# An f32 attention and two feed-forward layers on one core: batches 0 and 1 take the first layer in two rounds of 8 feature tiles, and GpSimd is preferred for the low halves

## The chip, the cores and the metric

The kernel runs on one core of a Trainium2 chip. The metric is the device time of one execution in microseconds (us). A core has five engines that matter here: TensorE (PE, matrix products), VectorE (DVE), ScalarE (ACT), GpSimd (POOL), and SyncE (SP), which here only issues transfers (DMA). Each engine works through its own instructions in the order in which they were written; semaphores hold an instruction back until what it needs is done, and all behind it on that engine wait with it.

## What is computed

For each of 4 batches (8 heads, 576 positions, head dimension 64) a Nystrom attention is formed; its result, 2304 tokens of 512, goes through two feed-forward layers with 2048 hidden features:

```python
A  = sm(q, k_lm);  Bm = sm(q_lm, k_lm);  C = sm(q_lm, k)     # softmax; _lm: means over 18 positions
Z  = Bm.T / (norm1(Bm) * norminf(Bm) + 1e-06)
for _ in range(6):
    Z = 2 * Z - Z @ Bm @ Z
x  = A @ Z @ C @ v                       # to (2304, 512)
h  = x @ w_in;   x = (h * cos(h)) @ w_out                       # first layer
h  = x @ w_in2;  x = (max(h, 0) + alpha * min(h, 0)) @ w_out2   # second layer
```

The weights of both layers are given as 64-bit floats, and the kernel turns them into 32-bit floats itself.

## The kernel before

**Precision.** Most large products are made from values split into a high half (rounded to TensorE's fast 32-bit form by an ACT copy) and a low half (value minus high half). Three products (high-high, high-low, low-high) make one. The subtraction that makes a low half is one two-input instruction on DVE or on POOL: line 323 (`sub`), whichever engine the planner picks.

**Weights.** A conversion (`convert`) takes a 128 x 512 piece. SP loads its raw words (512 KB) into one of three `raw` buffers (L464); DVE joins them by three instructions (L470, L472, L474). A piece of `w_in` then stays in one of eight `wi` buffers and is also written to a DRAM copy `w1d` (L497); a piece of `w_out` is split into halves (ACT L454, low half L323). The first layer needs 16 pieces of each, 32 conversions; 32 more make DRAM copies of the second layer's weights while the first layer runs.

**Attention.** Each batch has two `unit`s (two pairs of heads in each) and one `z_path` (the inverse). A unit of batch 1 to 3 loads k, q and v through the same three `raw` buffers (L551, L567, L568), transposes on PE (L593), takes landmark sums on DVE (L641), makes scores (L658), exponentials (L680), and C v (L703). `z_path` begins with small products (L767), iterates (L839, L852), and ends with L866. Its result goes with converted `w_in` into V' (`vprime`: PE L897, ACT L899, DVE L900), a 512 x 2048 matrix for each batch that stands for Z C v w_in. V' of batch 0 reads the `wi` buffers straight from the conversions; V' of the later batches reloads the pieces from `w1d` (L883).

**First layer.** It runs in 128 ticks (`tick`). A tick is one batch, one half of its positions (`ch`, 288 columns) and one tile of 128 features (`j`): the first product h (L937, six matmuls), ACT and DVE steps for h cos h (L942, L944, L946, L947, L948), its split (ACT L951, L323), and the second product (L964, twelve matmuls), which adds up over a round of feature tiles in four PSUM banks. At the end of a round the sums are written to the DRAM array `y1d` (L991); a second round loads the earlier sums (L977) and adds (L984). In batch 0 a round has 8 tiles, so its order is half 0 tiles 0-7, half 1 tiles 0-7, half 0 tiles 8-15, half 1 tiles 8-15. Batches 1 to 3 take one round of 16 tiles for each half. The table of ticks:

```python
ticks = [(0, ch, j) for jg in range(0, NF, JG) for ch in range(2) for j in range(jg, jg + JG)]
ticks += [(b, ch, j) for b in range(1, NB) for ch in range(2) for j in range(NF)]
```

with `NF` = 16 and `JG` = 8. Ticks 0 to 31 belong to batch 0, 32 to 63 to batch 1, and so on.

**Second layer.** It runs in chunks of 512 tokens with a seven-product scheme (L1208) and the products L1289, and the last chunk of 256 tokens plainly (L1253).

**What sets the order.** No order is written by hand. `Plan.go` goes through all operations with made-up durations (functions `pe`, `act`, `dve`, `pool`), due times (`tick_time`) and buffer slots, and writes each engine's instructions in the order that comes out. Constants stand in the table `KN`. Where an operation may go to DVE or POOL, it goes where the made-up end is earlier, less a bonus for POOL (`PB`). The work of a batch's attention is let in at a tick named in `KN` (`U0`), and the second layer's conversions begin at tick `C2`, one every `CD` ticks. A buffer tag has a fixed number of slots, used in turn, so that the raw piece number n waits until piece n-3 has been read.

Of the kernel before, what the change touches and what calls it, by code (L numbers as in the profile page):

```python
# [18 lines left out]
KN = dict(T0=46, TA=3.4, TBT=3.05, VE=4.0, U0=6, UD=7, UZ=24, C2=36, CD=2.6, LA=4, SW=6.0, BL=0.9, PB=0.2, AB=0.2, LM=126, JG=8, VG=8, AG=8, KA=0.004, KC=25, DRY=0)  # L19
# [239 lines left out]
def kernel(  # L259
# [13 lines left out]
    NB, H, S, D = q.shape  # L273
# [34 lines left out]
    def pool(n):  # L308
        return ("POOL", n / 480.0 + 0.15)
# [82 lines left out]
    g = Plan(place, rounded)  # L392
# [51 lines left out]
    valloc, cvops = [], []  # L444
    T0, TA, TBT = KN["T0"], KN["TA"], KN["TBT"]

    def tick_time(s):
        return T0 + TA * min(s, 2 * NF) + TBT * max(0, s - 2 * NF)
# [30 lines left out]
    gates = {}  # L479
# [436 lines left out]
    h1op = {}  # L916
# [4 lines left out]
    def tick(s):  # L921
        b, ch, j = ticks[s]
        T = tick_time(s)
        fb = j // 4
# [28 lines left out]
        jg = NF if b else JG  # L953
# [41 lines left out]
    LA = KN["LA"]  # L995
# [25 lines left out]
    n2 = 0  # L1021
    for s in range(NTK):
        b = s // (2 * NF)
        if s and s % (2 * NF) == 0:
            for fb in range(NFB):
                for c in range(2):
                    vprime(b, fb, c, tick_time(vfirst[b, fb]) - KN["VE"])
        tick(s)
        if s % (2 * NF) == KN["U0"] and b + 1 < NB:
            gates["ld"] = [h1op[s]]  # L1030
            t = 2 * NF * b
            for c in range(2):
                unit(2 * b + 2 + c, tick_time(s + KN["UD"] * (c + 1)))
            z_path(b + 1, tick_time(t + KN["UZ"]))
            gates["v"] = [g.ops[-1]]
# [6 lines left out]
    for (b, fb), o in vload.items():  # L1042
        o.after.append(h1op[max(0, vlast[b - 1, fb] - KN["VG"])])
# [311 lines left out]
```

## Time and profile before

| | |
|---|---|
| median of 3 runs | 901.36 us (897.68 to 902.41) |
| profiled execution | 894.15 us, span 892.3 us |
| PE busy | 829.2 us (93% of the span) |
| DVE busy | 643.4 us (72%) |
| ACT busy | 488.7 us (55%) |
| POOL busy | 167.9 us (19%) |

The span reaches from the first to the last instruction of the profiled execution; its time is 1.85 us longer. Busy shares are means over stages that are limited by different things, so the stages have to be read one by one: the 45.8 us before the first tick, the 128 ticks (45.8 to 495.5 us), and the second layer (495.5 to 892.3 us). The ticks' times are the starts of the first of their six matmuls on L937: tick 0 at 45.8 us, tick 4 at 58.9, tick 16 at 112.0, tick 24 at 159.0, tick 32 at 187.8, tick 64 at 295.8, tick 96 at 406.6.

### The profile page before, as it was taken

The page shows a single profiled execution, that of the slowest core. Times are in us where ns is not written, and L with a number is a line of the kernel's source. Part 1 is how long each engine was busy: PE and PEld are TensorE (multiplying, and loading weights), DVE is VectorE, ACT ScalarE, POOL GpSimd, SP SyncE. Part 2 cuts the span into 40 slices and gives each one's busy share as a digit, 9 for nine tenths or more (in the row PEclk, how much of TensorE's full clock was granted, in tenths as well). Part 3 has the DMA queues.
Part 4 walks back from the last instruction along what each step waited for, and adds up shares of the span by engine and source line. Part 5 has one row for each costly group of instructions (what it writes and reads, how often), then busy time and mean ns, then how long its engine had stood idle before and what let it go on. Part 6 is the DMA issues. An engine that isn't in the chain of part 4 may idle for free.

```text
span 892.3 us, 15368 instructions
## 1 busy us (share of the span) xinstructions
PE 829.2 (93%) x5681; PEld 728.4 (82%) x5681; DVE 643.4 (72%) x1251; ACT 488.7 (55%) x1132; POOL 167.9 (19%) x176
## 2 busy tenths in 40 slices
PE   6778948899989998999999989999999999999997
PEld 4447726798879887898889978989999998999996
DVE  4989877967798666987888687875565556555562
ACT  4466656667776677767778644443244334333431
POOL 1114211401123111233251122210120012000110
PEclk9899977999999999999999999999999999999999
DMA  8456674636735666558364211131104011310131
GB/s 229 142 189 155 176 235 161 199 100 153 178 121 203 231 131 152 155 195 260 125 203 155 94 47 49 60 104 51 36 32 111 24 36 60 84 36 24 59 119 24
DMA packets 89179, 109.28 MB, mean 122 GB/s; under 512 B 36112, under 2 KB 61200, under 8 KB 89104
## 3 DMA queue, kind: packets, MB, share of 16 engines
q1 hardware_dynamic: 89104, 108.30, 41.0%
q8 instruction: 45, 0.74, 0.3%
q14 instruction: 30, 0.25, 0.1%
HBM read 85.07 MB, written 23.20 MB: 121 GB/s over the span
## 4 chain that ended last, share of the span: by engine, by line
PE 63%; DVE 17%; DMA 9%; ACT 5%; issue 3%; SPq 1%; POOL 1%; DVEq 0%; ACTq 0%; POOLq 0%
PE acc L1289 20%; PE acc L964 12%; PE h L1208 9%; PE x L1208 7%; PE h L937 6%; DMA m<-in_moe_w_in_dram 4%; DMA m<-in_moe_w_out_dram 3%; DVE m L323 2%; DVE m L472 2%; PE x L897 2%; DVE m L474 2%; DVE m L948 2%; DVE m L470 2%; DVE m L944 1%; PE h L1253 1%
## 5 line engine op out<-in xcount | busy, mean ns | idle before, releaser
L964 PE MATMUL acc<-m,m 128*128 128x288 f32 x1536 | 236.5, 301 | 1.4 <-POOL m L323 1.1
L323 POOL TENSOR_TENSOR m<-m,m 128x288 fp32r<-128x288 f32 (+4 forms) x139 | 133.3, 966 | 521.7 <-ACT m L951 259.2
L964 PEld LDWEIGHTS acc<-m,m 128*128 128x128 f32 x1536 | 214.1, 190 | 13.6 <-issue 7.2
L1289 PE MATMUL acc<-m,m 128*128 128x512 f32 x864 | 206.7, 391 | 0.7 <-DVE m L323 0.4
L1289 PEld LDWEIGHTS acc<-m,m 128*128 128x128 f32 x864 | 158.3, 188 | 31.7 <-DVE m L323 0.9
L323 DVE TENSOR_TENSOR m<-m,m 128x512 fp32r<-128x512 f32 (+4 forms) x261 | 159.0, 632 | 32.4 <-ACT m L1157 9.5
L937 PE MATMUL h<-m,m 128*128 128x288 f32 x768 | 131.7, 308 | 15.4 <-DVE m L948 14.3
L937 PEld LDWEIGHTS h<-m,m 128*128 128x128 f32 x768 | 110.9, 193 | 32.4 <-DVE m L948 22.0
L1277 ACT ACTIVATE m<-m 128x512 fp32r<-128x512 f32 (+1 forms) x80 | 46.3, 589 | 111.9 <-DVE m L1275 109.4
L1208 PE MATMUL h<-m,m 128*128 128x256 f32 x768 | 106.5, 281 | 0.8 <-ACT m L318 0.7
L1208 PEld LDWEIGHTS h<-m,m 128*128 128x128 f32 x768 | 99.1, 188 | 3.7 <-ACT m L318 1.4
L1208 PE MATMUL x<-m,m 128*128 128x256 f32 x576 | 80.0, 283 | 1.8 <-ACT m L318 1.8
L1231 DVE TENSOR_TENSOR m<-h,m 128x512 f32<-128x512 f32 x32 | 22.1, 690 | 81.4 <-ACT m L318 78.5
L951 ACT ACTIVATE m<-m 128x288 fp32r<-128x288 f32 x128 | 56.4, 442 | 36.8 <-DVE m L948 34.6
L1208 PEld LDWEIGHTS x<-m,m 128*128 128x128 f32 x576 | 72.9, 188 | 3.5 <-ACT m L318 2.0
L318 ACT ACTIVATE m<-h 128x256 f32<-128x256 f32 (+2 forms) x93 | 36.9, 396 | 69.8 <-PE h L1208 58.3
L948 DVE SCALAR_TENSOR_TENSOR m<-m,h 128x288 f32<-128x288 f32 x128 | 57.1, 447 | 23.0 <-ACT m L947 23.0
L946 ACT ACTIVATE m<-m 128x288 f32<-128x288 f32 x128 | 56.3, 442 | 30.1 <-DVE m L944 29.2
L942 ACT ACTIVATE m<-h 128x288 int32<-128x288 f32 x128 | 51.8, 405 | 25.1 <-PE h L937 24.2
L1068 ACT ACTIVATE m<-m 128x512 fp32r<-128x512 f32 x68 | 41.4, 628 | 43.0 <-PE h L1208 18.7
L944 DVE SCALAR_TENSOR_TENSOR m<-h,m 128x288 f32<-128x288 f32 x128 | 57.4, 450 | 7.6 <-ACT m L942 7.1
L947 ACT ACTIVATE m<-m 128x288 f32<-128x288 f32 x128 | 55.8, 440 | 2.3
(149 smaller groups left out, 874.6 us busy)
## 6 DMA issues: line engine op xcount, KB each, us to landing
m<-in_moe_w_in_dram SPq DMA_DIRECT2D x32, 512.0 KB, 4.9
m<-in_moe_w_out_dram SPq DMA_DIRECT2D x32, 512.0 KB, 4.6
m<-wi2d SPq DMA_DIRECT2D x56, 256.0 KB, 3.3
m<-w1d SPq DMA_DIRECT2D x48, 256.0 KB, 5.0
y1d<-m SPq DMA_DIRECT2D x20, 288.0 KB, 4.2
out_dram<-m SPq DMA_DIRECT2D x36, 128.0 KB, 2.4
w1d<-m SPq DMA_DIRECT2D x16, 256.0 KB, 5.7
wi2d<-m SPq DMA_DIRECT2D x16, 256.0 KB, 2.6
```

What stands on the lines that cost most here:

```text
L323: ENG[e].tensor_tensor(o, a, b, op=ALU.subtract)
L937: nc.tensor.matmul(out=hp.t[:, 0:CW], lhsT=w_[:, js], rhs=x[:, cs], start=(i == 0), stop=(i == 5))
L942: op(act(CW, True), lambda e: nc.scalar.activation(k_.t, hp.t[:, 0:CW], AF.Copy, scale=INV2PI), r=[hp], w=[k_], target=T + 0.8)
L944: op(dve(CW), lambda e: nc.vector.scalar_tensor_tensor(u.t, hp.t[:, 0:CW], INV2PI, k_.t, op0=ALU.mult, op1=ALU.subtract), r=[hp, k_], w=[u])
L946: op(act(CW), lambda e: nc.scalar.activation(u.t, u.t, AF.Sin, scale=math.pi), rw=[u], aset="sin")
L947: op(act(CW), lambda e: nc.scalar.activation(u.t, u.t, AF.Square, scale=math.sqrt(2.0)), rw=[u])
L948: op(dve(CW), lambda e: nc.vector.scalar_tensor_tensor(hc.t, u.t, 1.0, hp.t[:, 0:CW], op0=ALU.subtract, op1=ALU.mult, reverse0=True), r=[h ...
L951: op(act(CW), lambda e: nc.scalar.activation(gh.t, hc.t, AF.Copy), r=[hc], w=[gh, gl])
L964: nc.tensor.matmul(out=yg[o].t[:, 0:CW], lhsT=w_.t[:, sl], rhs=x.t, start=(j == ja and i == 0), stop=(j == jb and i == 2),)
L1208: nc.tensor.matmul(out=rv(k), lhsT=a_.t[:, p, c2, js], rhs=b_.t[:, q_, c2, 0:hw], start=(first and c2 == 0 and i == 0), stop=(c2 == 1 and ...
L1277: op(act(w), lambda e, m_=m_, gh=gh: nc.scalar.activation(gh.t[:, 0:w], m_.t[:, 0:w], AF.Copy), r=[m_], w=[gh, gl])
L1289: nc.tensor.matmul(out=ya[n][t].t, lhsT=gv(x_), rhs=r_.t, start=(st and k == 0), stop=(en and k == 2))
```

## The change

Three things change. Batches 0 and 1 are interleaved in rounds of 8 tiles: tiles 0-7 of batch 0 (ticks 0-15), tiles 0-7 of batch 1 (16-31), tiles 8-15 of batch 0 (32-47), tiles 8-15 of batch 1 (48-63). Attention of batch 1 is let in before tick 0, and V' of both batches is made in two groups that read the conversions' own `wi` buffers, without the reload. The planner's bonus for POOL is 0.8 us instead of 0.2 (with POOL taken to be somewhat slower), and some due ticks are moved.

```diff
-KN = dict(... U0=6, UD=7, UZ=24, C2=36, CD=2.6, ... PB=0.2, ...)
+KN = dict(... U1=-1, U2=36, U3=66, UD=7, UZ=20, C2=48, CD=2.3, ... PB=0.8, ...)
...
     def pool(n):
-        return ("POOL", n / 480.0 + 0.15)
+        return ("POOL", n / 440.0 + 0.3)
...
     def tick_time(s):
-        return T0 + TA * min(s, 2 * NF) + TBT * max(0, s - 2 * NF)
+        return T0 + TA * min(s, 2 * JG) + TBT * max(0, s - 2 * JG)
...
     def vprime(b, fb, c, target):
-        if b:
+        if b > 1:
...
-    ticks = [(0, ch, j) for jg in range(0, NF, JG) for ch in range(2) for j in range(jg, jg + JG)]
-    ticks += [(b, ch, j) for b in range(1, NB) for ch in range(2) for j in range(NF)]
+    ticks = [(b, ch, j) for jg in range(0, NF, JG) for b in range(2) for ch in range(2) for j in range(jg, jg + JG)]
+    ticks += [(b, ch, j) for b in range(2, NB) for ch in range(2) for j in range(NF)]
...
-        jg = NF if b else JG
+        jg = JG if b < 2 else NF
...
+    def attend(b, s):
+        gates["ld"] = [h1op[s]] if s >= 0 else gates["ld"]
+        for c in range(2):
+            unit(2 * b + c, tick_time(s + KN["UD"] * (c + 1)))
+        z_path(b, tick_time(s + KN["UZ"]))
+        gates["v"] = [g.ops[-1]]
+
+    if KN["U1"] < 0:
+        attend(1, -1)
+        vgroup(1, range(FH))
     for s in range(NTK):
-        b = s // (2 * NF)
-        if s and s % (2 * NF) == 0:
-            for fb in range(NFB):
-                for c in range(2):
-                    vprime(b, fb, c, tick_time(vfirst[b, fb]) - KN["VE"])
+        if s == 4 * JG:
+            vgroup(0, range(FH, NFB))
+        if s == 6 * JG:
+            vgroup(1, range(FH, NFB))
+        if s >= 4 * NF and s % (2 * NF) == 0:
+            vgroup(s // (2 * NF), range(NFB))
         tick(s)
```

`vgroup(b, fbs)` calls `vprime` for the named groups of 512 features. The changed file's line numbers are higher by 1 (from L464 on) up to 16 (in the second layer).

How instructions move is seen in three places. The first is SP's list around the last load of the first half of `w_in`, before (m_157 holds the raw buffers, m_419 and m_442 are `wi` buffers):

```order
L464 DMA m_157<-in_moe_w_in_dram 128x1024
L464 DMA m_157<-in_moe_w_out_dram 128x1024 x2
L497 DMA w1d<-m_419 128x512 x2
L497 DMA w1d<-m_442 128x512
L464 DMA m_157<-in_moe_w_out_dram 128x1024
L497 DMA w1d<-m_442 128x512
L464 DMA m_157<-in_moe_w_out_dram 128x1024 x4
L1185 DMA alpha_sb<-in_moe_alpha_dram 128x16x1
L551 DMA m_157<-in_k_dram 64x9x64 x4
```

The same place in the changed kernel (m_408 is a `wi` buffer):

```order
L465 DMA m_157<-in_moe_w_in_dram 128x1024
L552 DMA m_157<-in_k_dram 64x9x64 x4
L465 DMA m_157<-in_moe_w_out_dram 128x1024
L552 DMA m_157<-in_q_dram 64x9x64 x4
L498 DMA w1d<-m_408 128x512
L465 DMA m_157<-in_moe_w_out_dram 128x1024 x2
L568 DMA m_157<-in_v_dram 64x2x320
L569 DMA m_157<-in_v_dram 64x2x256
```

The loads of batch 1's k, q and v have moved ahead of most of the `w_out` pieces: k now stands where the first `w_out` load stood, and seven `w_out` loads came ahead of it before.

The second place is PE's list at the end of batch 1's `z_path`, before (m_207 is a `wi` buffer, m_408 the result of `z_path`, m_415 and m_425 the attention of batch 0):

```order
L852 MATMUL x<-m_69 128x64 x2
L937 MATMUL h<-m_415,m_1011 128x288
...
L866 MATMUL x<-m_69 128x128 x2
L964 MATMUL acc<-m_474,m_1463 128x288 x12
L897 MATMUL x<-m_207,m_408 64x512 x2
L964 MATMUL acc<-m_474,m_1463 128x288 x12
L937 MATMUL h<-m_415,m_1011 128x288
```

and in the changed kernel (m_812 and m_1158 are the attention of batch 1):

```order
L867 MATMUL x<-m_69 128x128 x2
L965 MATMUL acc<-m_485,m_750 128x288 x6
L898 MATMUL x<-m_207,m_410 64x512
L898 MATMUL x<-m_283,m_410 64x512 x2
L898 MATMUL x<-m_207,m_410 64x512
L965 MATMUL acc<-m_485,m_750 128x288 x6
L898 MATMUL x<-m_408,m_410 64x512 x2
L938 MATMUL h<-m_812,m_1240 128x288 x3
L938 MATMUL h<-m_1158,m_1240 128x288 x3
```

Before, the end of `z_path` stands between ticks 25 and 26, and ticks of batch 0 follow it. Now it stands right ahead of tick 16, and no tick of batch 0 is left to run behind it: tick 16 is the first that reads batch 1.

The third place is DVE's list in the changed kernel behind that end (L858 is the last step of the `z_path` on DVE, L901 the low half of V', L471 and L473 the first two steps of a conversion), with what each waits for:

```order
L858 TENSOR_SCALAR m_69<-m_69 128x2x64
L901 TENSOR_TENSOR m_1240<-x,m_1240 128x512 [waits Activation_49]
L471 TENSOR_SCALAR m_207<-m_157 128x512 [waits DMAHW1_49,PE_49]
L901 TENSOR_TENSOR m_1240<-x,m_1240 128x512 [waits Activation_49]
L471 TENSOR_SCALAR m_207<-m_157 128x512 [waits DMAHW2_49]
L471 TENSOR_SCALAR m_283<-m_157 128x512 [waits DMAHW6_49,DMAHW7_49,DMAHW5_49,DMAHW0_49]
L473 SCALAR_TENSOR_TENSOR m_207<-m_157,m_207 128x512 [waits DVE_49]
```

The first conversion of the second half of `w_in` writes the `wi` buffer m_207 and waits for PE, that is for V' of batch 1 to have read it. Before, that buffer was free once V' of batch 0 had read it, near tick 0.

## Rows read from the trace of the kernel before

**Rows 1.** Busy time in stretches: us, PE, PEld, DVE, ACT, POOL, clock, DMA share, GB/s.

```profile
45.80:58.90 13.10, 9.31 (x34) 5.05 (x32) 11.12 (x25) 7.52 (x16) 0.00 (x0) 0.87 0.49 154
58.90:112.00 53.10, 47.52 (x355) 40.65 (x355) 49.30 (x90) 35.95 (x87) 17.86 (x16) 1.00 0.66 181
112.00:159.00 47.00, 29.70 (x208) 21.14 (x206) 37.02 (x81) 29.60 (x65) 8.84 (x9) 0.78 0.61 193
159.00:187.80 28.80, 27.03 (x177) 24.70 (x178) 24.88 (x49) 17.90 (x44) 7.12 (x7) 0.94 0.56 185
187.80:295.80 108.00, 104.02 (x815) 91.64 (x815) 85.46 (x183) 76.43 (x185) 23.52 (x24) 1.00 0.55 157
295.80:406.60 110.80, 105.88 (x817) 93.33 (x816) 84.01 (x181) 80.02 (x194) 23.59 (x25) 0.98 0.61 166
406.60:495.50 88.90, 85.76 (x602) 79.74 (x601) 73.43 (x141) 68.17 (x174) 28.48 (x31) 0.98 0.58 189
495.50:892.30 396.80, 388.46 (x2450) 351.18 (x2448) 245.52 (x420) 153.01 (x330) 52.04 (x51) 1.00 0.19 57
```

**Rows 2.** Waits of PE between 45.8 and 187.8 us: us in total, times, longest.

```profile
PE x L767 <- ACT m L680: 9.0, 1, 9.0
PE h L937 <- DVE m L948: 5.2, 6, 1.3
PE x L688 <- DVE m L900: 3.7, 1, 3.7
```

**Rows 3.** DVE's groups by shape between 45.8 and 187.8 us: count, busy us, mean ns.

```profile
L474 DVE SCALAR_TENSOR_TENSOR m<-m,m 128x512 int32<-128x512 int32 x28 | 22.3, 802 | 0.1
L472 DVE SCALAR_TENSOR_TENSOR m<-m,m 128x512 int32<-128x512 int32 x28 | 20.5, 734 | 0.0
L470 DVE TENSOR_SCALAR m<-m 128x512 int32<-128x512 int32 x27 | 14.0, 523 | 6.3 <-DMA m<-in_moe_w_out_dram 3.9 <-DMA m<-in_moe_w_in_dram 2.4
L948 DVE SCALAR_TENSOR_TENSOR m<-m,h 128x288 f32<-128x288 f32 x31 | 13.7, 446 | 2.5 <-ACT m L947 2.5
L323 DVE TENSOR_TENSOR m<-m,m 128x512 fp32r<-128x512 f32 x12 | 8.2, 685 | 0.6 <-ACT m L454 0.5
L323 DVE TENSOR_TENSOR m<-m,m 128x288 fp32r<-128x288 f32 x8 | 3.5, 453 | 0.6 <-ACT m L951 0.4
```

**Rows 4.** POOL's groups by shape between 45.8 and 187.8 us.

```profile
L323 POOL TENSOR_TENSOR m<-m,m 128x288 fp32r<-128x288 f32 x23 | 23.2, 1012 | 77.6 <-ACT m L951 72.2 <-PE acc L964 2.8 <-issue 2.6
L323 POOL TENSOR_TENSOR m<-m,m 128x512 fp32r<-128x512 f32 x4 | 6.1, 1524 | 11.5 <-DMA w1d<-m 8.7 <-ACT m L454 1.5 <-DMA m<-in_moe_w_out_dram 1.3
```

**Rows 5.** Timelines of DVE, then POOL, 66 to 78 us: start, duration.

```profile
67.44 0.41 DVE L470 TENSOR_SCALAR m<-m 128x512 int32<-128x512 int32 x1
...
68.14 0.68 DVE L472 SCALAR_TENSOR_TENSOR m<-m,m 128x512 int32<-128x512 int32 x1
68.74 1.48 DVE L470 TENSOR_SCALAR m<-m 128x512 int32<-128x512 int32 x1
70.14 1.29 DVE L474 SCALAR_TENSOR_TENSOR m<-m,m 128x512 int32<-128x512 int32 x1
...
68.26 2.63 POOL L323 TENSOR_TENSOR m<-m,m 128x512 fp32r<-128x512 f32 x2 [1.30 <-ACT m L454]
```

**Rows 6.** Timeline of SP: two `w_out` loads, then batch 1's first k load.

```profile
51.65 0.93 SPq L464 DMA_DIRECT2D m<-in_moe_w_out_dram  x2
...
74.25 3.42 SPq L551 DMA_DIRECT2D m<-in_k_dram  x4
```

**Rows 7.** Timeline of PE, 160 to 195 us: end of `z_path`, V', steady ticks.

```profile
166.35 1.06 PE L866 MATMUL x<-m 128*128 128x128 f32 x4
...
169.30 1.27 PE L897 MATMUL x<-m,m 128*64 128x512 f32 x4
...
173.10 1.08 PE L897 MATMUL x<-m,m 128*64 128x512 f32 x4
...
190.13 0.95 PE L937 MATMUL h<-m,m 128*128 128x288 f32 x6
...
192.53 0.95 PE L937 MATMUL h<-m,m 128*128 128x288 f32 x6
```

More of the change, by code (lines that the diff above doesn't have):

```diff
@@ L18 @@
 INV2PI = 1.0 / (2.0 * math.pi)
-KN = dict(T0=46, TA=3.4, TBT=3.05, VE=4.0, U0=6, UD=7, UZ=24, C2=36, CD=2.6, LA=4, SW=6.0, BL=0.9, PB=0.2, AB=0.2, LM=126, JG=8, VG=8, AG=8, KA=0.004, KC=25, DRY=0)
+KN = dict(T0=46, TA=3.4, TBT=3.05, VE=4.0, U1=-1, U2=36, U3=66, UD=7, UZ=20, C2=48, CD=2.3, LA=4, SW=6.0, BL=0.9, PB=0.8, AB=0.2, LM=126, JG=8, VG=8, AG=8, KA=0.004, KC=25, DRY=0)
 ADJ = {}
@@ L444 @@
     valloc, cvops = [], []
+    JG = KN["JG"]
     T0, TA, TBT = KN["T0"], KN["TA"], KN["TBT"]
     def tick_time(s):
-        return T0 + TA * min(s, 2 * NF) + TBT * max(0, s - 2 * NF)
+        return T0 + TA * min(s, 2 * JG) + TBT * max(0, s - 2 * JG)
     def loads(n, fn, dur, r=(), w=(), target=None, after=(), rw=(), hold=()):
@@ L1002, with vgroup @@
     gates["v"] = []
-    for fb in range(NFB):
-        for c in range(2):
-            vprime(0, fb, c, tick_time(vfirst[0, fb]) - KN["VE"])
+    def vgroup(b, fbs):
+        for fb in fbs:
+            for c in range(2):
+                vprime(b, fb, c, tick_time(vfirst[b, fb]) - KN["VE"])
+    FH = JG // 4
+    vgroup(0, range(FH))
     w2c = {}
@@ L1021 @@
     n2 = 0
-    for s in range(NTK):
-        b = s // (2 * NF)
-        if s and s % (2 * NF) == 0:
-            for fb in range(NFB):
-                for c in range(2):
-                    vprime(b, fb, c, tick_time(vfirst[b, fb]) - KN["VE"])
-        tick(s)
[L1029 to L1035, printed above, removed]
+    US = {KN["U1"]: 1, KN["U2"]: 2, KN["U3"]: 3}
+    def attend(b, s):
+        gates["ld"] = [h1op[s]] if s >= 0 else gates["ld"]
+        for c in range(2):
+            unit(2 * b + c, tick_time(s + KN["UD"] * (c + 1)))
[4 more added lines that the diff above has]
+        vgroup(1, range(FH))
+    for s in range(NTK):
+        if s == 4 * JG:
[4 more added lines that the diff above has]
+            vgroup(s // (2 * NF), range(NFB))
+        tick(s)
+        if s in US:
+            attend(US[s], s)
+            if US[s] == 1:
+                vgroup(1, range(FH))
         while n2 < len(w2) and int(KN["C2"] + KN["CD"] * n2) <= s:
@@ L1042 @@
     for (b, fb), o in vload.items():
-        o.after.append(h1op[max(0, vlast[b - 1, fb] - KN["VG"])])
+        o.after.append(h1op[max(0, vlast[b - 1 if b > 2 else 0 if fb < FH else 1, fb % FH + FH if b == 2 else fb] - KN["VG"])])
     HF = DFF // 2
```

## The prediction, made before the changed kernel ran

> **What bounds the kernel now.** I read first the busy times of the stretches between ticks [rows 1]. From tick 32 on PE is what counts: it is busy 104.0 of 108.0 us in ticks 32-63, 191.6 of 199.7 in ticks 64-127, and 388.5 of 396.8 in the second layer. Ticks 0-31 are different. They take 13.1 + 53.1 + 47.0 + 28.8 = 142.0 us, and PE is busy 113.6 of them; ticks 32-63, as many, take 108.0. DVE is busy 11.1 + 49.3 + 37.0 + 24.9 = 122.3 of the 142.0 us, and 49.3 of 53.1 in ticks 4-15, where it is the bound.
>
> Then I read who keeps PE waiting there [rows 2]. The longest wait, 9.0 us, is that of the first product of batch 1's `z_path` for an exponential on ACT; the next single one, 3.7 us, is for a low half of V' on DVE. Both are attention or V' of the next batch standing in PE's list ahead of ticks that could run. The shape groups of DVE [rows 3] say what it works on: 28 conversions in the stretch, at 0.523 + 0.734 + 0.802 = 2.06 us each, are 57 of its 122 us. So in ticks 0-31 the kernel converts the second half of both weights, because tick 16 already needs it, and does the attention of batch 1 beside it.
>
> **What the change takes from DVE in ticks 0-31.** Counted in the order of both kernels, from tick 0's L948 to tick 32's: conversions 25 before, 21 after (the rest follow tick 32); low halves 512 wide on DVE 12 before, 2 after (four more on POOL, six put off with their conversions); low halves 288 wide on DVE 9 before, 11 after. With [rows 3]: -4 x 2.06 - 10 x 0.685 + 2 x 0.453 = -14.2 us.
>
> **What POOL costs in return.** In ticks 0-31 POOL gets four more wide low halves and two fewer narrow ones: 4 x 1.524 - 2 x 1.012 = +4.1 us [rows 4]. This is not free to DVE. L470 takes 0.41 us and L472 0.68 with POOL idle, but L470 takes 1.48 and L474 1.29 while POOL works on two low halves from 68.26 us [rows 5]. Over the stretch the three steps of a conversion are 0.11 + 0.05 + 0.12 = 0.29 us longer than alone (0.41, 0.68, 0.68, L474 taken as L472), 28 times, 8.1 us, for 17.9 + 8.8 + 7.1 = 33.8 us of POOL: 0.24 us of DVE lost for each us of POOL. L948, with an input in PSUM, stays at 0.446 us. So +4.1 us of POOL costs DVE 1.0 us; 4.1 us if all of it blocked, nothing if all fell into DVE's gaps. I take 1.0, the mean of the stretch.
>
> The Trainium skill (SBUF — State Buffer, Who interferes with whom) says that a DVE instruction with two SBUF inputs and a GpSimd one that reads SBUF exclude each other and that the second "fully blocks". The trace agrees where they meet (1.29 against 0.68 us). By it alone, with every moved half blocking, the change would lose most of its gain; that is rival 2.
>
> With DVE's idle time as it is (142.0 - 122.3 = 19.7 us), ticks 0-31 get 14.2 - 1.0 = 13.2 us shorter.
>
> **Which wait is next.** Attention of batch 1 must now end before tick 16, not tick 32, since no tick of batch 0 stands behind it. So I work the stretch out a second way, along that chain. Its first k load now stands where the first `w_out` load stood, issued at 51.65 us; before it was issued at 74.25 [rows 6]. From there to the first V' matmul at 169.30 [rows 7] it took 95 us. Over those 95 us DVE was busy about 0.93 x 37.8 + 37.0 + 0.86 x 10.3 = 81 us [rows 1]. What stands in DVE's list of the changed kernel between the two ends (every instruction at its shape's mean, less 11%, by which neighbours overlapped in those 95 us) comes to about 62 us, 19 less, chiefly because 9 conversions lie there and not 17 (8 x 2.06 = 16.5). If the chain shortens by those 19 us it takes 76, and V' of batch 1 starts at 51.65 + 76 = 128 us. Bounds: 51.65 + 62/0.93 = 118, where DVE's work alone counts, and 51.65 + 95 = 147, where the chain takes as long as now. I take 128, since DVE's queue ended most of the links before. Tick 16 then starts at about 131, behind two V' pairs on PE (1.27 + 1.08 [rows 7]) and a low half on DVE; before it started at 112.0.
>
> Ticks 16-31 then lack nothing but the second half of `w_in`, whose conversion waits for V' of batch 1 to give its buffers back. DVE: 10 conversions (20.6), 16 x 2 steps at 0.446 (14.3), 6 narrow and 3 wide low halves (4.8): 39.7 us, at 0.93 busy 43. PE: 16 x 2.40 (190.13 to 192.53, [rows 7]) + 3 V' pairs at 1.08 = 41.6 us, less some second products that slip behind tick 32. I take 42, so tick 32 starts at 173 and not 187.8: 14.8 us gained. The two ways agree; I take 14.5.
>
> **What is moved later or costs nothing.** Ticks 32-63: 11 conversions lie there before and after, V' and attention of batch 2 too, and PE has the same products to do; it was busy 104.0 of 108.0, so 0, with -4 to +4 as bounds (its idle time gone, or doubled). Batch 1's second round adds 4 loads and 4 stores of `y1d`, and 8 additions on DVE in place of copies (8 x 0.446 = 3.6 us, hidden, since DVE is busy 79% there; without that cover, 3.6). The 16 reloads of `w1d` that go were hidden behind PE. Ticks 64-127: 25 conversions, 21 before (+8.2 us of DVE); 22 more narrow halves on POOL (-10.0 on DVE, +22.3 on POOL, which costs DVE 0.24 x 22.3 = 5.3). DVE gets +3.5 on 157.4 of 199.7 us, with PE idle 8.1: I take +1, bounds -3 and +6. Second layer: two dozen wide halves move to POOL, each 1.524 - 0.685 = 0.84 us later, before products that PE reaches through a queue it is 98% busy with: 0, bounds 0 and +5.
>
> **The sum.** -14.5 + 0 + 1 + 0 = -13.5 us against the profiled execution's 894.15: 880.6. That execution lies 7.2 us below the median of 901.36, so on the scale of the medians: 901.36 - 13.5 = 888.
>
> **Rivals.** *1, larger gain:* DVE packs as well over all of ticks 0-31 as in ticks 4-15 (0.93). 122.3 - 13.2 = 109.1 / 0.93 = 117 us and not 142: -25, so 877. For it: the 13.4 us of the two long waits of PE go if the order is kinder. Against: attention is a serial chain.
>
> *2, no change through POOL:* every moved half blocks DVE for its whole time. Ticks 0-31 then lose 4.1 and not 1.0, and ticks 64-127 22.3 - 10.0 + 8.2 = +20.5 us of DVE, which fills 178 of 199.7 us (89%) and pushes PE by about 8. Sum -11 + 8 = -3, 898. For it the row at 70.14 us; against it the mean of 0.24.
>
> *3, slower:* the chain of batch 1's attention keeps its 95 us. V' starts at 147, tick 16 at 150, tick 32 at 192, 4 us later than now; with +1 behind it, +5, 906. It decides from a V' of about 142 us on. For it: most of its links are waits on other engines, and k, q, v and `w_out` share three raw buffers in turn. Against: DVE has 19 us less ahead of it.
>
> *4:* the gain is there but the moved conversions cost as much in ticks 32-127 (+4 and +6): -14.5 + 10 = -4.5, 897.
>
> **Chances.** Forecast (881 to 894) 0.51; rival 1 (870 to 881) 0.20; rivals 2 and 4 (894 to 900) 0.18; rival 3 0.11. A difference under 0.5% (4.5 us) is about what a measurement of this kernel cannot tell from none. Faster than 896.9: 0.51 + 0.20 + 0.05 of the third case = 0.76; within: 0.13 of it and 0.02 of rival 3 = 0.15; slower 0.09. The range leaves out half of rival 3 and half of rival 1's far end: 874 to 901.
>
> **What would show it.** In the changed profile: tick 16 (the first h that reads batch 1) at 131 us, give or take 8; tick 32 near 173; ticks 16-31 in 40 to 45 us without the clock falling to 0.78; PE's 9.0 us wait on the exponential gone or much shorter; ticks 32-63 in 104 to 112 us; the second layer in 397. POOL's busy time goes up by about 80 us, and L472 and L474 get longer. Wrong would be: a wait of 10 us or more right ahead of V' of batch 1, or ticks 64-127 longer than 204 us.

## The result, and the profile after

Against the kernel before on the same chip the changed kernel took 888.6 us (median of 4, 888.1 to 889.3) where the kernel before took 899.5 (median of 4): a ratio of 0.9896, 95% interval 0.9855 to 0.9936. A second comparison, with more executions (10 of the changed kernel, 33 of the kernel before), gave 891.7 against 898.0, 0.9938 (0.9915 to 0.9962). So the change is faster, by 6 to 11 us (0.6 to 1.0%); 13.5 were predicted.

The first view is that of the busy times between ticks of the changed kernel (888.11 us, span 886.1). Columns as in [rows 1]; the cuts are ticks 0, 4, 16, 32, 64, 96, and the end of the last tick's first steps.

```profile
46.70:58.80 12.10, 8.40 (x36) 4.33 (x35) 10.55 (x21) 7.89 (x18) 0.81 (x1) 1.00 0.55 135
58.80:133.40 74.60, 61.55 (x473) 50.72 (x471) 60.62 (x126) 47.93 (x109) 22.30 (x21) 0.93 0.50 133
133.40:175.70 42.30, 38.45 (x264) 34.17 (x263) 36.47 (x71) 29.17 (x73) 9.91 (x11) 1.00 0.65 203
175.70:285.70 110.00, 105.46 (x817) 91.96 (x816) 92.56 (x191) 84.00 (x199) 33.17 (x34) 1.00 0.53 156
285.70:395.90 110.20, 105.04 (x815) 91.84 (x815) 85.71 (x181) 77.93 (x188) 29.93 (x34) 1.00 0.67 187
395.90:488.10 92.20, 86.81 (x603) 79.91 (x602) 77.26 (x139) 67.97 (x174) 41.26 (x42) 0.98 0.61 200
488.10:886.10 398.00, 389.62 (x2449) 352.66 (x2448) 236.05 (x384) 152.95 (x330) 93.17 (x88) 1.00 0.19 57
```

Read as a balance against [rows 1]: before tick 0 46.7 us against 45.8, +0.9. Ticks 0-31 12.1 + 74.6 + 42.3 = 129.0 against 142.0, -13.0. Ticks 32-63 110.0 against 108.0, +2.0. Ticks 64-95 110.2 against 110.8, -0.6. From tick 96 to the end 92.2 + 398.0 = 490.2 against 88.9 + 396.8 = 485.7, +4.5. The sum is -6.2, the difference of the two spans. Of the 13.0 us that ticks 0-31 gain, 5.9 are spent again behind them.

PE's waits between 46.7 and 175.7 us, to be held against [rows 2]:

```profile
PE h L938 <- DVE m L949: 9.4, 10, 2.2
PE x L594 <- DMA m<-in_q_dram: 3.7, 2, 2.4
PE x L898 <- DVE m L475: 3.0, 2, 1.5
PE x L768 <- DVE m L731: 0.9, 1, 0.9
```

The single wait of 9.0 us ahead of `z_path` is down to 0.9. What has grown are the short waits for the last DVE step of a tick (L949): 9.4 us in ten waits, where [rows 2] has 5.2 in six. Two waits for q of batch 1 make 3.7 us. None is longer than 2.4 us.

DVE's groups by shape in the same stretch, then POOL's, against [rows 3, 4]:

```profile
L473 DVE SCALAR_TENSOR_TENSOR m<-m,m 128x512 int32<-128x512 int32 x23 | 18.2, 800 | 0.1
L475 DVE SCALAR_TENSOR_TENSOR m<-m,m 128x512 int32<-128x512 int32 x22 | 16.8, 776 | 0.0
...
L471 DVE TENSOR_SCALAR m<-m 128x512 int32<-128x512 int32 x21 | 10.4, 500 | 6.6 <-DMA m<-in_moe_w_in_dram 4.2 <-DMA m<-in_moe_w_out_dram 1.2 <-issue 1.1
...
L323 DVE TENSOR_TENSOR m<-m,m 128x288 fp32r<-128x288 f32 x10 | 6.7, 679 | 1.7 <-ACT m L952 1.7
...
L323 POOL TENSOR_TENSOR m<-m,m 128x288 fp32r<-128x288 f32 x21 | 18.6, 891 | 79.3 <-ACT m L952 70.4 <-PE x L689 5.7 <-DMA m<-in_k_dram 2.9
L323 POOL TENSOR_TENSOR m<-m,m 128x512 fp32r<-128x512 f32 x8 | 10.3, 1286 | 15.3 <-ACT m L455 9.8 <-DMA m<-in_q_dram 4.9 <-PE acc L965 0.6
```

Some 22 conversions stand here where 28 stood. A low half of 288 columns takes 0.679 us on DVE on average, but that mean mixes two kinds. The five that POOL's work overlapped for 41 to 76% of their time took 0.53 to 1.32 us; the other five took 0.44 to 0.46, as one does when POOL is idle (0.449, below). Before, none of the eight on DVE met any work of POOL (0.453).

The end of batch 1's chain on PE, against [rows 7]: the first V' product at 129.54 us and tick 16 (L938) at 133.41.

```profile
129.54 1.94 PE L898 MATMUL x<-m,m 128*64 128x512 f32 x8
...
133.41 0.80 PE L938 MATMUL h<-m,m 128*128 128x288 f32 x4
```

### The profile page after: what moved, and what is told of

Same layout as the page of the kernel before. It is cut to its first block, busy times and chain, and to the rows that moved or that the text cites. A ratio compares the mean times of both kernels' runs of the same rounds, so it can differ in the third digit from the quotient of the medians.

```text
span 886.1 us, 15408 instructions
## 1 busy us (share of the span) xinstructions
PE 826.8 (93%) x5681; PEld 726.6 (82%) x5681; DVE 632.6 (71%) x1191; ACT 487.9 (55%) x1132; POOL 239.6 (27%) x246
## 4 chain that ended last, share of the span: by engine, by line
PE 57%; DVE 20%; DMA 10%; ACT 6%; issue 4%; SPq 2%; POOL 1%; DVEq 0%; ACTq 0%
PE acc L1305 21%; PE h L1224 9%; PE acc L965 9%; PE x L1224 7%; PE h L938 4%; DMA m<-in_moe_w_in_dram 4%; DVE m L323 3%; DMA m<-in_moe_w_out_dram 3%; DVE m L473 2%; DVE m L475 2%; DVE m L945 2%; DVE m L949 2%; DVE m L471 2%; PE x L898 1%; ACT m L318 1%
## 5 line engine op out<-in xcount | busy, mean ns | idle before, releaser
L323 POOL TENSOR_TENSOR m<-m,m 128x288 fp32r<-128x288 f32 (+4 forms) x211 | 207.7, 989 | 559.6 <-ACT m L952 240.0
L323 DVE TENSOR_TENSOR m<-m,m 128x512 fp32r<-128x512 f32 (+4 forms) x189 | 138.0, 751 | 26.1 <-ACT m L1173 7.1
L938 PE MATMUL h<-m,m 128*128 128x288 f32 x768 | 129.9, 305 | 21.5 <-DVE m L949 19.3
L938 PEld LDWEIGHTS h<-m,m 128*128 128x128 f32 x768 | 107.7, 188 | 41.0 <-DVE m L949 28.1
L1224 PEld LDWEIGHTS h<-m,m 128*128 128x128 f32 x768 | 100.1, 190 | 6.5 <-ACT m L318 4.1
L949 DVE SCALAR_TENSOR_TENSOR m<-m,h 128x288 f32<-128x288 f32 x128 | 56.8, 446 | 24.6 <-ACT m L948 15.3
```

The lines of the kernel that those rows point to most:

```text
L323: ENG[e].tensor_tensor(o, a, b, op=ALU.subtract)
L938: nc.tensor.matmul(out=hp.t[:, 0:CW], lhsT=w_[:, js], rhs=x[:, cs], start=(i == 0), stop=(i == 5))
L949: op(dve(CW), lambda e: nc.vector.scalar_tensor_tensor(hc.t, u.t, 1.0, hp.t[:, 0:CW], op0=ALU.subtract, op1=ALU.mult, reverse0=True), r=[h ...
L1224: nc.tensor.matmul(out=rv(k), lhsT=a_.t[:, p, c2, js], rhs=b_.t[:, q_, c2, 0:hw], start=(first and c2 == 0 and i == 0), stop=(c2 == 1 and ...
```

## The experiments

Stretches are given as in the balance above: ticks 0-31, 32-63, 64-127 (to the start of tick 127), and from there to the end. For the kernel before they are 141.9, 108.1, 197.3 and 399.2 us. They come from one execution each, the ratios from all; executions of one kernel scatter by some 1%, so a stretch is trusted here where several kernels show the same. Four profiles whose instructions stand in the same order up to tick 32 (the changed kernel twice, and two kernels below that differ from it only later) took 127.3, 129.0, 129.4 and 130.3 us for ticks 0-31. So 3 us in that stretch of a single profile can be scatter.

**The two halves of the change apart.** First the changed kernel once more:

> The changed kernel again, beside the others on one chip. Both theories: 886 to 890 us, 0.985 to 0.993 of the kernel before; its profile with tick 16 at 131 to 136 us and tick 32 at 173 to 178 us.

130.3, 110.1, 202.0 and 399.9 us; 891.7 us, 0.9938. The time, the ratio and tick 32 (178.4 us) each lie just above the range that was expected. Its windows from tick 0 to the end, cut at ticks 16, 32, 64 and 127:

```profile
48.10:135.90 87.80, 72.82 (x508) 57.13 (x506) 70.34 (x146) 55.93 (x126) 23.47 (x22) 0.90 0.50 132
135.90:178.40 42.50, 38.37 (x263) 34.07 (x262) 36.49 (x71) 29.06 (x73) 10.40 (x11) 1.00 0.65 202
178.40:288.50 110.10, 105.59 (x816) 91.94 (x815) 92.31 (x191) 84.05 (x199) 32.99 (x34) 1.00 0.53 156
288.50:490.50 202.00, 188.41 (x1398) 167.90 (x1397) 160.68 (x316) 143.37 (x356) 69.75 (x75) 1.00 0.64 192
490.50:890.40 399.90, 391.00 (x2468) 353.86 (x2466) 236.42 (x387) 155.17 (x335) 94.86 (x90) 1.00 0.20 58
```

Then the rounds with GpSimd's old bonus and price:

```diff
-KN = dict(... PB=0.8, ...)
+KN = dict(... PB=0.2, ...)
-        return ("POOL", n / 440.0 + 0.3)
+        return ("POOL", n / 480.0 + 0.15)
```

> Rounds, early attention and moved conversions as in the changed kernel, but GpSimd's bonus 0.2 us and its made-up cost as before. My theory (the gain is made by the order of ticks 0 to 31, GpSimd moves little): tick 32 within 3 us of the changed kernel's 175.7, time within 4 us of the changed kernel's, so 0.985 to 0.995 of before. Rival (the gain comes from the low halves that DVE no longer makes): tick 32 at 182 or later, time 0.994 to 1.003 of before.

892.6 us, 0.9958 (0.9935 to 0.9982). The windows of this kernel from tick 0 to tick 127:

```profile
44.90:132.80 87.90, 70.90 (x510) 57.37 (x508) 74.23 (x155) 55.77 (x128) 13.75 (x13) 0.92 0.52 132
132.80:178.80 46.00, 40.75 (x260) 36.75 (x259) 39.95 (x80) 30.29 (x74) 9.69 (x9) 0.93 0.63 198
178.80:285.00 106.20, 103.81 (x817) 91.81 (x816) 89.27 (x194) 83.17 (x196) 20.96 (x24) 1.00 0.56 156
285.00:492.50 207.50, 190.05 (x1398) 168.07 (x1397) 169.00 (x340) 147.61 (x360) 53.71 (x57) 1.00 0.63 187
```

The rounds alone shorten ticks 0-31 by 8 us (133.9) and ticks 32-63 by 2, and lengthen ticks 64-127 by 10 (207.5): DVE is busy 169.0 us there, and PE, with the same products as in the other kernels, idles 17. The ratio lies in the rival's range and just outside mine, tick 32 (178.8 us) near mine and far from the rival's. The ratio's interval overlaps that of the changed kernel, so the totals do not show that GpSimd's part adds anything to the rounds.

And GpSimd's part without the rounds (the kernel before, with `PB=0.8` and the new price):

> The kernel before with GpSimd's bonus 0.8 us and its new made-up cost, and no other change. My theory: tick 32 within 4 us of 187.8, time 0.996 to 1.004 of before. Rival (the gain comes from the low halves that DVE no longer makes): tick 32 at 180 or earlier, time 0.993 or less.

900.2 us, 1.0041 (1.0019 to 1.0063): slower, if by little. 139.4, 108.0, 201.7 and 400.2 us: it wins 2.5 us early and loses 4.4 in ticks 64-127. Tick 32 (186.5 us) and the time are where my theory had them. So the gain of the whole change comes from the rounds and what goes with them.

**All low halves on DVE** (`PB=-9.0` in the changed kernel, so that POOL makes only four of them):

> The changed kernel with a malus of 9 us on GpSimd, so that nearly every low half is made on DVE. My theory (a us of GpSimd costs DVE about 0.24 us, so moving a half does pay): the steps of a conversion fall to about 0.41, 0.68 and 0.68 us; DVE gets 7 us more to do in ticks 0 to 31, tick 32 at 179 to 185; ticks 32 to 127 3 to 12 us longer; time 5 to 18 us over the changed kernel's. Rival (a half on GpSimd blocks DVE for its whole time, so moving it gains nothing): tick 32 at 173 to 177, time within 3 us of the changed kernel's.

893.7 us, 0.9955 (0.9933 to 0.9977): 2 us above the changed kernel by the medians, and the intervals overlap. Its windows:

```profile
47.90:135.10 87.20, 73.12 (x515) 58.37 (x515) 74.33 (x164) 54.86 (x133) 1.86 (x2) 0.90 0.54 142
135.10:173.40 38.30, 35.55 (x255) 32.73 (x254) 34.62 (x77) 28.22 (x71) 0.00 (x0) 1.00 0.59 193
173.40:287.50 114.10, 106.65 (x816) 93.78 (x816) 101.09 (x229) 85.83 (x200) 0.00 (x0) 0.97 0.54 158
287.50:496.30 208.80, 190.27 (x1401) 170.57 (x1401) 172.38 (x393) 149.16 (x357) 1.91 (x2) 0.98 0.63 187
496.30:892.40 396.10, 389.43 (x2464) 353.14 (x2463) 251.09 (x472) 155.43 (x337) 0.00 (x0) 1.00 0.20 58
```

I had expected ticks 0-31 to lengthen. They are 5 us shorter than in the changed kernel (125.5 against 130.3, and still 2 us below the shortest of the four above), with DVE busy only 2 us more (108.9 against 106.8). Tick 32, at 173.4, and the total are where the rival had them, not I. But those 5 us are lent: ticks 32-63 take 114.1 us (PE has the same 816 products there, at a granted clock of 0.97 against 1.00), and tick 64 stands 239.6 us behind tick 0, as it does with rounds alone (240.1) and in the changed kernel (240.4). Ticks 64-127 are 6.8 us longer (208.8), the second layer 3.8 us shorter. With rounds, then, no low halves on POOL, the old share and the new one gave 0.9955, 0.9958 and 0.9938: the gain of the rounds does not hang on POOL.

**Batch 1's attention let in later** (changed kernel, `U1=4` for `U1=-1`):

> The changed kernel with one number changed: batch 1's attention is let in after tick 4 instead of ahead of tick 0. Theory (the chain from batch 1's first k load to its V' sets tick 16, with some 76 us however much DVE has to do beside it): the load moves later by some 7 to 12 us, so V' of batch 1 and tick 16 come at 140 to 146 us (133 to 136 in the changed kernel), ticks 0-15 grow by 5 to 9 us, tick 32 is up to 7 us later, the total 2 to 6 us above the changed kernel (ratio to the kernel before 0.996 to 1.001, where the changed one had 0.994). Rival (DVE's sum of work in ticks 0-31 sets tick 32, wherever the chain stands): tick 32 within 2 us of the changed kernel's 178, the total within 1.5 us of it.

890.7 us, 0.9921 (0.9891 to 0.9952), not to be told from the changed kernel. The first k load on SP and the first V' product on PE in this kernel:

```profile
62.69 2.59 SPq L552 DMA_DIRECT2D m<-in_k_dram  x4
131.90 1.94 PE L898 MATMUL x<-m,m 128*64 128x512 f32 x8
```

and in the second profile of the changed kernel:

```profile
52.98 2.84 SPq L552 DMA_DIRECT2D m<-in_k_dram  x4
132.01 1.94 PE L898 MATMUL x<-m,m 128*64 128x512 f32 x8
```

The load comes 9.7 us later and V' at the same time, not at 140 or later, as I had expected. So the chain from k to V' has no length of its own of 76 us: it takes 69 us with the late load and 79 with the early one. Tick 32 (176.8 us) and the total are where the rival had them, by which DVE's sum of work sets them.

**Halves placed by stretch** (low halves on DVE alone in ticks 0-31 and in the second layer, POOL preferred only between):

```diff
-        op([pool(CW), dve(CW)], lambda e: sub(e, gl.t, hc.t, f32(gh.t)), r=[hc, gh], w=[gl])
+        op(dve(CW) if s < 32 else [pool(CW), dve(CW)], lambda e: sub(e, gl.t, hc.t, f32(gh.t)), r=[hc, gh], w=[gl])
...
     def either(n):
-        return [pool(n), dve(n)]
+        return dve(n)
```

and likewise for the halves of attention 0 and 1, of the `w_out` pieces and of the second layer.

> The changed kernel with the low halves placed by stretch: on DVE alone in ticks 0-31 (first-layer h and w_out halves, attention of batches 0 and 1) and in the second layer, on GpSimd by preference only in ticks 32-127. Theory (what GpSimd takes over in ticks 0-31 comes too late and slows DVE, in the second layer likewise, while in ticks 32-127 it relieves DVE): start to tick 32 as with all halves on DVE (173, against 178 for the changed kernel), ticks 32-127 as in the changed kernel (312 us, not 323), second layer 396: the total 6 to 9 us below the changed kernel, ratio to the kernel before 0.984 to 0.988. Rival (the gain to tick 32 is lent only: what is not done on GpSimd early is due later): within 2 us of the changed kernel, ratio 0.992 to 0.996.

883.4 us (6 executions), 0.9828 (0.9796 to 0.9859): faster than before and than the changed kernel, whose interval begins at 0.9915 (at 0.9855 in the first comparison, where the two just touch). Windows from tick 0 to the end:

```profile
48.60:138.60 90.00, 73.44 (x514) 58.44 (x514) 77.71 (x175) 56.48 (x125) 0.00 (x0) 0.89 0.54 138
138.60:177.70 39.10, 36.90 (x257) 33.23 (x256) 35.41 (x80) 29.24 (x73) 0.00 (x0) 1.00 0.58 190
177.70:284.40 106.70, 104.36 (x813) 91.30 (x812) 93.75 (x199) 84.60 (x198) 29.28 (x30) 1.00 0.58 166
284.40:485.80 201.40, 190.49 (x1404) 168.92 (x1403) 162.81 (x327) 144.77 (x358) 58.94 (x64) 1.00 0.64 193
485.80:881.90 396.10, 389.24 (x2462) 352.87 (x2460) 250.42 (x469) 155.27 (x337) 2.42 (x3) 1.00 0.19 58
```

The total came where the theory had it, the stretches not quite: ticks 0-31 take 129.1, hardly less than 130.3, and 3.4 us are won in ticks 32-63 instead. Tick 64 stands 235.8 us behind tick 0, 3 to 5 us earlier than in the two profiles of the changed kernel (239.0 and 240.4). DVE is busy 77.71 + 35.41 = 113.1 us in ticks 0-31, 6.3 more than there, with 22 conversions in both. POOL made 21 narrow and 8 wide halves there, 21 x 0.449 + 8 x 0.683 = 14.9 us of DVE's time, and four steps of the attention 576 wide, 0.75 us each on DVE: 17.9 us. So POOL's help relieves DVE of a third of what it takes over, and brings no earlier tick 32.

**The second layer alone** (only its halves on DVE):

> The changed kernel with the low halves of the second layer alone on DVE; the first layer stays as changed. It divides the gain of the placed kernel (883.4 us, ratio 0.983) between the second layer and ticks 0-31. Theory (the two parts add up): second layer 396 us instead of 400, everything before it as in the changed kernel, so 3 to 4 us below it, ratio 0.988 to 0.991; the other half of the placed kernel's gain then belongs to ticks 0-63. Rival 1 (second layer alone does it): ratio 0.982 to 0.985. Rival 2 (the second layer's 4 us come from what the first layer leaves behind, not from its own halves): the second layer stays at 399 to 401 us and the ratio at 0.992 to 0.996.

884.9 us, 0.9862 (0.9828 to 0.9897), between the ranges of the theory and of rival 1; 129.4, 110.2, 201.4 and 396.0 us. Up to tick 96 its instructions run as in the changed kernel; behind it, nine halves of the first layer's last ticks leave POOL as well. So the second layer's halves are the larger part of what placement brings, and rival 2 is out. Whether ticks 0-31 add to it can't be told from the totals, whose intervals overlap; for it speaks only tick 64, 239.6 us behind tick 0 here and 235.8 above (235.7 in one more kernel with that placement, below). PE's waits from tick 127 to the end show part of the 4 us. First the changed kernel, then this one:

```profile
PE h L1224 <- ACT m L318: 3.3, 4, 2.3
PE h L1224 <- DVE m L320: 0.4, 1, 0.4
```

```profile
PE acc L1305 <- DVE m L323: 1.4, 1, 1.4
```

These are 3.7 us against 1.4; the other 1.5 are busy time of PE (391.0 against 389.5). Cut at the same counts of PE's products, the first quarter of the layer takes 32.0 + 48.0 = 80.0 us in the changed kernel and 30.4 + 46.7 = 77.1 here, the rest 312.6 and 312.1. So the loss is at the layer's start, where PE waits for ACT's steps. That these are late because of a late half on POOL is argued, not shown.

**The same placement in the kernel before:**

> The kernel before (whole batches one after the other, GpSimd's old price and preference) with the same placement of the low halves as in the kernel named placed: DVE alone in ticks 0-31 and in the second layer. Theory (rounds and placement are worth something apart): ticks 0-31 within 3 us of before, since their bound is the two chains of attention and conversions; DVE there gets more to do but is slowed less; second layer 1 to 3 us shorter; ratio 0.995 to 1.000. Rival (placement is worth the same 5 us with either order of ticks): ticks 0-31 some 5 us shorter and the ratio 0.988 to 0.993. If they get longer by over 4 us, DVE's sum of work sets that stretch in the kernel before and GpSimd's share of it is of use there.

895.1 us, 0.9963 (0.9943 to 0.9984); 140.0, 110.4, 196.7 and 396.0 us. The ratio is in the theory's range; the rival's 5 us did not come. The second layer again gives 3.2 us, ticks 0-31 1.9, and ticks 32-63 take 2.3 back. In all profiles taken, the second layer takes 396.0 to 396.4 us with its halves on DVE (seven) and 399.2 to 400.4 with 52 to 95 us of POOL work in it (the other seven).

Ticks 0-31 divide the same way. DVE is idle 13 to 17 us of them in the six kernels with at most two low halves on POOL there (15.9 here, 16.0 in the placed kernel), and 20 to 24 us in the eight others, with either order of ticks. So what POOL takes off DVE's busy time there comes back as time in which DVE waits.

**When the second layer's conversions run.** The changed kernel with `C2=36, CD=2.6`, as before:

> The changed kernel with the conversions of the second layer's weight let in from tick 36 on every 2.6 ticks, as before the change, instead of from tick 48 every 2.3. Theory (part of the gain of ticks 0-31 is given back in ticks 64-127 because more conversions lie there, 25 against 21): ticks 64-127 drop from 202 us towards the 197 of the kernel before, ticks 32-63 grow by less than 2 us; total 2 to 4 us below the changed kernel, ratio 0.989 to 0.992. Rival (it does not matter where they lie, since DVE has the same sum of them from tick 32 on): ticks 32-63 grow by as much as ticks 64-127 shrink, the total within 1.5 us of the changed kernel.

896.8 us, 0.9987 (0.9965 to 1.0009): nearly all of the gain is lost. I had expected a gain or no difference. The window of ticks 32-63 of this kernel:

```profile
174.90:290.10 115.20, 106.62 (x815) 91.92 (x815) 101.66 (x210) 80.79 (x191) 36.12 (x35) 1.00 0.61 176
```

DVE is busy 101.7 of 115.2 us there (92.3 of 110.1 with the later conversions), and ticks 64-127 win only 1.4 us back. The profiled execution, at 892.2 us the fastest of twelve, shows none of the loss: its span is the 890.4 us of the changed kernel, since its ticks 0-31 took 3.0 us less, with the same instructions. So ticks 32-63, 5.1 us longer, are the likeliest place of the loss of the median; one profile does not show it.

And the placed kernel with still later ones (`C2=56, CD=2.05`):

> The placed kernel with the conversions of the second layer's weight let in later still, from tick 56 on every 2.05 ticks instead of from tick 48 every 2.3. Letting them in from tick 36 lost the changed kernel 4 to 5 us, chiefly in ticks 32-63 (115 us instead of 110). Theory (ticks 32-63 are where DVE is short, since what ticks 0-31 put off falls due there): ticks 32-63 drop by 0 to 2 us from 106.7, ticks 64-127 grow by 2 to 6 us, since 34 conversions must now fit in 71 ticks; total 0 to 5 us above the placed kernel, ratio 0.983 to 0.988. Rival (the later the better, DVE has room to the end of the first layer): total 2 to 4 us below the placed kernel, ratio 0.978 to 0.981.

889.6 us, 0.9931 (0.9907 to 0.9956): 6 us worse than the placed kernel, more than the theory allowed, and against the rival. Ticks 0-63 stay (tick 64 235.7 us behind tick 0), ticks 64-127 take 210.9 instead of 201.4, with 29 conversions and not 25. Of those 9.5 us, 5.7 are busy time of PE, at a granted clock of 0.98 where it was 1.00. So the start at tick 48 lies between two losses, the early one measured in the changed kernel, the late one in the placed.

**What POOL's work costs DVE.** To the kernel with all halves on DVE one needless piece of POOL work is added in each tick, in one kernel a subtraction of two SBUF tiles, in the other three fills that read nothing, both into a tile that is dead by then:

```diff
+        def extra(e):
+            nc.gpsimd.tensor_tensor(hc.t, hc.t, f32(gh.t), op=ALU.subtract)
+        op(pool(CW), extra, r=[gh], rw=[hc])
```

> The kernel with nearly all halves on DVE, plus one needless GpSimd instruction in each tick of the first layer: it subtracts two 288-wide tiles in SBUF into a tile that is dead by then (it adds work and leaves no part of the computation out). Nobody waits for its result but the next writer of that buffer. Theory (GpSimd's reads of SBUF hold up DVE's instructions with two SBUF inputs): some 0.85 us of GpSimd a tick, 27 us to tick 32; the three steps of a conversion, 0.339 + 0.683 + 0.702 us on average to tick 32 without it, come to 0.25 to 0.4 us longer together, the low halves 288 wide, 0.45 us, likewise longer by some 0.05; the steps that read PSUM (relu and sum) stay. Ticks 0-31 grow by 5 to 9 us and ticks 32-127 by 10 to 25 us. Rival (the cost in the changed kernel was GpSimd's late results, not its reads): durations on DVE stay within 3% and the stretches within 2 us.

> The same as the kernel with the extra GpSimd reads, in the same order of instructions, but the added GpSimd work of each tick is three fills of the dead 288-wide tile, which read nothing (nothing of the computation is left out). Theory (it is GpSimd's reads, against instructions with two SBUF inputs, that hold DVE up): the steps of a conversion within 3% of those with no GpSimd work (0.339, 0.683, 0.702 us to tick 32) and the stretches within 2 us of that kernel's. Rival (any work of GpSimd on SBUF slows DVE, or the wait for the buffer does): DVE's steps or the ticks get longer here as well, by at least half of what the reads cost per us of GpSimd.

898.8 us, 1.0042 (1.0016 to 1.0069), with the reads; 894.9, 0.9966 (0.9931 to 1.0002), with the fills; 893.7, 0.9955, with neither. DVE's groups to tick 127 without the added work:

```profile
L949 DVE SCALAR_TENSOR_TENSOR m<-m,h 128x288 f32<-128x288 f32 x126 | 56.0, 446 | 10.1 <-ACT m L948 9.5
L323 DVE TENSOR_TENSOR m<-m,m 128x288 fp32r<-128x288 f32 x124 | 55.4, 449 | 6.6 <-ACT m L952 5.7
...
L473 DVE SCALAR_TENSOR_TENSOR m<-m,m 128x512 int32<-128x512 int32 x64 | 43.6, 683 | 0.2
L471 DVE TENSOR_SCALAR m<-m 128x512 int32<-128x512 int32 x64 | 26.7, 422 | 21.4 <-DMA m<-in_moe_w_in_dram 11.5 <-DMA m<-in_moe_w_out_dram 6.5 <-DMA m<-in_q_dram 1.6
...
L323 DVE TENSOR_TENSOR m<-m,m 128x512 fp32r<-128x512 f32 x33 | 22.5, 682 | 1.8 <-ACT m L1084 1.1 <-ACT m L455 0.4
```

with the reads (the last line is POOL's):

```profile
L323 DVE TENSOR_TENSOR m<-m,m 128x288 fp32r<-128x288 f32 x124 | 59.3, 482 | 7.4 <-ACT m L952 6.2
L949 DVE SCALAR_TENSOR_TENSOR m<-m,h 128x288 f32<-128x288 f32 x126 | 56.2, 447 | 9.2 <-ACT m L948 6.1 <-POOL m L955 1.9
L473 DVE SCALAR_TENSOR_TENSOR m<-m,m 128x512 int32<-128x512 int32 x64 | 46.7, 732 | 0.2
...
L471 DVE TENSOR_SCALAR m<-m 128x512 int32<-128x512 int32 x64 | 31.8, 501 | 17.6 <-DMA m<-in_moe_w_in_dram 11.3 <-DMA m<-in_moe_w_out_dram 6.4
...
L323 DVE TENSOR_TENSOR m<-m,m 128x512 fp32r<-128x512 f32 x33 | 25.2, 764 | 1.9 <-ACT m L1087 1.6
...
L955 POOL TENSOR_TENSOR m<-m,m 128x288 f32<-128x288 f32 x125 | 118.1, 947 | 372.4 <-DVE m L323 292.8 <-ACT m L947 24.9 <-DVE m L714 11.2
```

and with the fills:

```profile
L473 DVE SCALAR_TENSOR_TENSOR m<-m,m 128x512 int32<-128x512 int32 x64 | 43.7, 685 | 0.2
...
L471 DVE TENSOR_SCALAR m<-m 128x512 int32<-128x512 int32 x64 | 27.8, 439 | 19.5 <-DMA m<-in_moe_w_in_dram 12.8 <-DMA m<-in_moe_w_out_dram 6.6
...
L955 POOL MEMSET m<- 128x288 f32 x375 | 130.8, 351 | 359.1 <-DVE m L323 284.6 <-ACT m L947 27.2 <-DVE m L714 10.1
```

118 us of POOL reads lengthen L471, L473, L475 (43.9 to 45.8), the narrow halves and the wide ones by 5.1 + 3.1 + 1.9 + 3.9 + 2.7 = 16.7 us, 0.14 us for each; 131 us of fills lengthen L471 by 1.1 us and the four others by 0.1 at most (the narrow halves take 0.451 us). L949, with an input in PSUM, stays at 0.446 to 0.449. Which instructions suffer was much as expected. The size was not: ticks 0-31 take 125.6 and 125.1 us, not 130 or more, and the total pays 5 us for the reads (8 by the ratios) where 15 to 34 were expected.

The reads cost more than the fills by the totals, 3.9 us with the intervals apart. The single profiles do not show it: ticks 64-127 take 212.4 us with the reads and 211.9 with the fills, against 208.8 with neither, and in both PE is busy 4 to 5 us longer, at a granted clock of 0.96 and 0.95 against 0.98. So there the rival of the second expectation, that POOL's work lengthens the ticks whatever it is, is not excluded.

The Trainium skill (SBUF — State Buffer, Who interferes with whom) says that a DVE instruction with two SBUF inputs contends with a GpSimd one that reads SBUF, not with one that only writes it, and that one in a two-port mode contends with GpSimd. For two inputs these rows agree: such steps lengthen by the reads (0.683 to 0.732) and not by the fills (0.685). L471 has a single input and lengthens by both (0.422 to 0.501 and to 0.439); that it runs in a two-port mode no row shows. All its 64 took 0.405 to 0.430 us with neither; with the reads 13 of them took longer, up to 1.03, with the fills 11, up to 0.68.

## Why the prediction was right, and where its steps were not

The number, 888.0, met the median of 888.6, but it was a gain of 13.5 us taken from a median of 901.4, and the medians of later executions of the kernel before are 897.5 to 899.5. The gain measured is 6 to 11 us, and in the spans of the two profiled executions 6.2. So that the number was met so closely is in part luck: a gain too large was taken from a base too high. Point by point:

- **What the change takes from DVE in ticks 0-31** (-14.2, less 1.0). DVE's busy time went from 122.3 to 10.55 + 60.62 + 36.47 = 107.6 us, -14.7, and the stretch from 142.0 to 129.0, -13.0 for 13.2 predicted. Right in size, and DVE's idle time stayed about as it was, as the prediction took it. Without more GpSimd the stretch is 133.9, so the rounds make about two thirds of its gain.
- **What POOL costs in return.** POOL did not grow there: 0.81 + 22.30 + 9.91 = 33.0 us, 33.8 before, since its halves became shorter (0.891 and 1.286 us for 1.012 and 1.524). Per us the price was met: (0.500 - 0.422 + 0.800 - 0.683 + 0.776 - 0.683) x 22 + (0.679 - 0.449) x 10 = 8.6 us for 33.0, 0.26 where I had 0.24. But 2.3 of these 8.6 are narrow halves that DVE made beside POOL, and before there were none of these. The 0.68 us of L472 that the prediction read as the time with POOL idle (68.14 to 68.82 in [rows 5]) lie beside POOL's work from 68.26 on; the value holds all the same (0.683 with all halves on DVE). The price is no constant, as the added reads show (0.14).
- **Which wait is next.** V' at 129.5 (128), tick 16 at 133.4 (131), ticks 16-31 42.3 us (42) with the clock at 1.00, tick 32 at 175.7 (173). The numbers held and the reason did not: started 9.7 us later, the chain ends at the same time. Nor does DVE's sum alone set it: ticks 0-15 take 86 to 90 us in all kernels with this order, with 70 to 78 us of DVE. DVE and PE are each busy 80 to 88% there, and what sets the rest stays open: the chain of work followed back from tick 16 to tick 4 is mixed, with PE's second products 16% of it in two profiles with the same instructions, and next to them the load of q (9%) in the first and the loads of `w_out` (16%) in the other. Rival 3 (95 us for the chain) is out.
- **What is moved later.** This is the step that was mis-sized: 0 and +1 for ticks 32-63 and 64-127 measured +2.0 and +2.7 (200.0 against 197.3), in the second profile +2.0 and +4.7, and the second layer 0 measured +1.2 and +0.7, all inside their bounds and all on the same side. That is rival 4's forecast at about half to two thirds of its price. By the time at which they ran, ticks 0-31, 32-63 and 64-127 held 28, 10 and 22 conversions before and 22, 13 and 25 after; that these make the loss is argued from the counts. Letting the second layer's conversions in early again did not remove it: ticks 32-127 took 315.8 us then, 312.1 in the changed kernel, 305.4 before. Rounds alone show it most (+10 in ticks 64-127, -2 in ticks 32-63); GpSimd's preference wins back 5.5 in ticks 64-127. In the second layer I had costed the wide halves on POOL at nothing, hidden by PE's queue. They are not hidden: the layer would take 396 us with its halves on DVE, and most of the 4 us are lost in its first 80. The old share of POOL loses nearly as much there (399.4 us), so the preference itself costs 1 us there at most.
- **Rival 1** did not come: DVE's idle time in the stretch stayed about as it was (21.4 us, 19.7 before). **Rival 2**, every moved half blocking DVE, comes two thirds of the way in ticks 0-31, where work on POOL that is worth 17.9 us of DVE relieves it of 6.3, but not in ticks 64-127, where POOL's relief is worth 6.8 us in single profiles (202.0 against 208.8).
- **Of the signs named**, POOL's busy time rose by 71.7 us (80), L473 got longer (0.734 to 0.800), L475 did not (0.802 to 0.776).

## What to carry to other kernels

A gain in an early stretch has to be followed to the end: work that is only put off comes due in the stretch whose cover is thinnest, so compare the times of several later marks, not the first one. Where a second engine slows the first, try its share of the work stretch by stretch: here POOL's halves won time in ticks 64-127, none in ticks 0-31, where DVE is no less busy, and lost 4 us in the second layer. Placing the halves so was worth 1.1% (0.9938 to 0.9828), more than the change itself in the same measure (0.6%), and most of that came from the second layer. And set a predicted gain against a median of many executions: three of them moved ours by 3 us.

## What was not expected of the hardware

POOL's fills are almost free for DVE (1.1 us lost to 131 us of them), its two-input subtractions are not (16.7 us lost to 118), and the price for each us of POOL's work ran from 0.14 to 0.26 us; what sets it was not tried. POOL pays as well: of its added subtractions of 288 columns, the 7 that met no DVE work took 0.801 us, the 60 that lay wholly beside it 1.02 on average.
